# Block 1 of x normalised as columns, and a first row tile that is turned twice

## The chip, the cores and the metric

The kernel runs on one core of one Trainium2 chip. The metric is the device time of one execution in microseconds (us); lower is better. TensorE (PE) multiplies, VectorE (DVE) and ScalarE (ACT) work elementwise, GpSimd (POOL) does a few elementwise passes, and SyncE (SP) issues most of the DMA transfers; ScalarE and GpSimd issue some as well.

## The reference

An attention branch and a gated feed-forward branch run over the same normalised input, and their product is added to the input. `x` has 2048 rows of 512 numbers in f32; there are 32 heads of 16; the feed-forward width is 1792.

```python
xn = _layernorm(x, axis=-1)                       # mean and variance over the 512 columns, eps 1e-5
s  = _A_ref(xn, wqkv, wo)                         # softmax attention over all 2048 rows, then @ wo
g  = _silu(_B_ref(xn, w_gate, w_up, w_down))      # (silu(xn @ w_gate) * (xn @ w_up)) @ w_down
return x + s * g
```

## The kernel before

The kernel has an opening of some 150 us, in which `xn` and the queries, keys and values are made, and a long main part, in which attention and the feed-forward products are interleaved on TensorE by a plan written out ahead. The order on every engine is the order in which the program issues (a manual schedule); each engine's queue and each DMA queue is served in that order, and tiles carry the waits.

**Precision.** Products that need nearly full f32 use two parts: `hi`, a value rounded to fp32r, and `lo`, the rest. A product is then three products: hi by hi, lo by hi, hi by lo. So each operand of the opening is copied into a `hi` part by ScalarE and subtracted into a `lo` part by VectorE (x) or GpSimd (weights; `high_w` at L574, `low_w` at L578).

**Blocks and slots.** `x` is worked through in four blocks of 512 rows, block `b` from 0 to 3, each of four row tiles of 128 rows (`NT = 4`). A block takes twelve slots: eight feature tiles (`feature_tile`: queries and keys, 128 features by 512 rows each) and four value tiles (`value_tile`: 128 rows by 512 features). Each slot is twelve products of 128x512 on TensorE (`project`, L718 and L720) into one of four PSUM buffers `ps`, which ScalarE and VectorE empty: a feature tile as squares (`top` or `sq`, L770), `hi` (L771) and `lo` (L772), which SP's queue stores (`q_d`, `k_d`, L774) from a `parts` tile of four buffers; a value tile by a copy into `vt` (L797). In block 0 the value tiles come first (slots 0 to 3, features in slots 4 to 11); in the later blocks the feature tiles do. Slots are counted through: slot 12 is the first of block 1. The weights of a slot are loaded five slots ahead and split two slots ahead.

**Two ways to the transposed x.** The products need `xn` with its 512 columns on the partitions, in `xt[b % 2]`, as `hi` and `lo`.

- *By turning* (blocks 0 and 1 before the change): rows are loaded into `xin` (the tile `facc`), VectorE takes mean and variance (`stats`, L615 to L620), `rates` makes the reciprocal deviation `rs` (a root on ScalarE, L624, and a few tiny VectorE operations, L627 to L633), `norm` (L638) subtracts the mean and multiplies by the rate into `xn[t]`, TensorE turns it in four transposes (`turn`, L643) into a bank, `acc` or `extra`, and `split_x` takes `hi` (ScalarE, L652) and `lo` (VectorE, L655) from there. `turn_x` does turn and split.
- *By columns* (blocks 2 and 3): a second copy of `x`, already transposed, is an input (`xcols`). `columns_of` loads the block's rows for the statistics alone, and the columns themselves; `rates_x` makes means and rates; `spread_mr` turns these 8 rows with one transpose (L680), copies them (ScalarE, L681) and writes them to DRAM (`mr_d`, ScalarE's queue, L682); `load_mr` (L685) reads them back broadcast to all partitions into `wide_mr` (0.5 MB); then for each quarter of the columns VectorE subtracts and multiplies (L673), ScalarE makes `hi` and VectorE `lo` (L673 too: those are steps that the same line issues). `store_x` keeps the result in DRAM for the feed-forward part (`xt_d`, GpSimd's queue, L664).

`step(at, late, ...)` books such a piece for slot `at`, ahead of the slot's products (`late` 0) or behind them (1). The tuple given to `columns_of` holds the slots: load of rows, load of columns, statistics, rates, spread, first normalised quarter, and the delays of the `lo` parts and of the store.

**The first row tile.** To let TensorE start early, value tile 0 is not made from `hi` and `lo`, but in one pass of plain f32: row tile 0 is normalised in two halves, turned into four banks, copied to `xf` (L741) and multiplied by the raw weights (`first_tile`, L755; in the middle of it, row tile 1 is turned). `xf` is split into `xt` later, in slot 2. Ahead of it TensorE is kept busy by products of a tile of zeros (`busy`, L583). The chain of the first tile is: load, statistics, rate, normalisation, turn, copy, products.

**Copies for the feed-forward part.** `copy_fx` (L811, ScalarE) copies block 0's `xt` into `fx` in 16 pieces, one a slot.

Of the kernel before, what the change touches and what calls it, by code (L numbers as in the profile page):

```python
# [19 lines left out]
P = 128  # L20
# [99 lines left out]
def tile_block(ctx: ExitStack, tc: tile.TileContext, x, xcols, wqkv, wo, w_gate, w_up, w_down, out):  # L120
# [401 lines left out]
    with ExitStack() as pro:  # L522
# [13 lines left out]
        def load_tile(t):  # L536
            if t:
                sp.dma_start(xin[:, t % NT], x[t * P:(t + 1) * P])
            else:
                for engine, w in zip((nc.scalar, sp), wide):  # L540
                    engine.dma_start(xin[:, t, w], x[t * P:(t + 1) * P, w])

        def load_x(b):
            for t in range(NT):
                load_tile(b * NT + t)

        load_tile(0)
        busy = pc.tile([P, P], F32, name="busy")
        dve.memset(busy, 0.0)
# [29 lines left out]

        worder = [8, 9, 10, 11, 0, 1, 2, 3, 4, 5, 6, 7]  # L580

        for _ in range(11):
            mm(extra[:, :P], busy, busy, start=True, stop=True)  # L583
        for kind, i in ((load_w, 8), (load_tile, 1), (load_w, 9), (load_w, 10), (load_tile, 2), (load_w, 11),
                        (load_tile, 3), (load_w, 0)):
# [70 lines left out]

        def turn_x(b, t, between=None):
            split_x(b, t, turn(t), between)
            if t == NT - 1 and b:
                store_x(b)  # L660

        def store_x(b):
            for j in range(2):
                pool.dma_start(xt_d[b, j], xt[b % 2][j].bitcast(F32))  # L664
# [3 lines left out]
        def step(at, late, make, *what):  # L668
            steps.setdefault((at, late), []).append(partial(make, *what))
# [12 lines left out]
            nc.scalar.dma_start(mr_d[b].rearrange("s t p -> (s t) p"), rows_mr)  # L682

        def load_mr(b):
            sp.dma_start(wide_mr, mr_d[b].rearrange("s t p -> s (t p)")[None].to_broadcast([P, 2, TB]))  # L685

        def columns_of(b, rows, cols, ats):
            load, turned, counted, rated, spread, normed, lows = ats
            block = slice(b * TB, (b + 1) * TB)
            step(load, 0, sp.dma_start, rows, x[block].rearrange("(t p) d -> p t d", p=P))  # L690
            step(turned, 0, sp.dma_start, cols, xcols[:, block].rearrange("(c p) t -> p c t", p=P))
            for t in range(NT):
                step(counted + t // 2, 0, stats, t, rows)
            step(rated, 0, rates_x)
            step(spread, 0, spread_mr, b)
            step(spread + 1, 0, load_mr, b)
            hi, lo = xt[b % 2]
            for c in range(DT):
                raw = cols[:, c]
                step(normed + c, 0, dve.tensor_sub, raw, raw, wide_mr[:, 0])  # L700
                step(normed + c, 0, dve.tensor_mul, raw, raw, wide_mr[:, 1])
                step(normed + c, 1, nc.scalar.copy, hi[:, c], raw)
                step(normed + lows[c], 1, dve.tensor_sub, lo[:, c], raw, hi[:, c].bitcast(F32))
            step(normed + lows[-1], 1, store_x, b)
# [22 lines left out]


        stats(0)
        rates(0, 1)  # L730
        made = norm(0, wide)
        high_w(8)
        tc.add_manual_dep(low_w(8).ins, made.ins.name, settled, reason="GpSimd would hold VectorE up")
        xf = one.tile([P, DT, P], F32, tag="th", name="xf")
# [2 lines left out]
        for c, to in enumerate((acc, bankx, extra, banky)):  # L737
# [2 lines left out]
                rates(1, 2)  # L740
            nc.scalar.copy(xf[:, c], to[:, c * P:(c + 1) * P])  # L741
        made = norm(1)
        for c in range(1, DT):
            high_w(8 + c)
            part = low_w(8 + c)
            if c == 1:
                tc.add_manual_dep(part.ins, made.ins.name, settled, reason="GpSimd would hold VectorE up")
# [34 lines left out]
        def value_tile(b, t):  # L782
            xh, xl = xt[b % 2]
            order = None
            if b == 0:
                parts = [slice(i, i + 1) for i in range(3)] if t == 1 else [slice(0, 3, 2), slice(1, 2)]
                order = [(i, part) for part in parts for i in range(DT)]
                if t == 1:
                    order.insert(11, (partial(turn_x, 0, 2), None))
            if b == t == 0:  # L790
                ps = first_tile()
            else:
                ps = project([(vh[:, c], vl[:, c], c) for c in range(DT)], xh, xl, slice(t * P, (t + 1) * P), order,
                             extra if b == t == NB - 1 else None)
            if b == 0 and t == 1:
                turn_x(0, 3)
            nc.scalar.copy(vt5[:, :, t, :, :DH], ps.rearrange("p (g h d) -> p g h d", g=NG, h=4))  # L797
            if b < NB - 1 and t == NT - 1:
                store_v(pool, b, 0, NT)
            elif b == NB - 1 and t == 1:  # L800
                store_v(sp, b, 0, 2)
            elif b == NB - 1 and t == NT - 1:
                return partial(store_v, sp, b, 2, NT)
# [6 lines left out]
            dst = fx[halves[h], j].rearrange("p (c u) t -> u p c t", u=2)[u]  # L810
            nc.scalar.copy(dst[:, 2 * w:2 * w + 2], xt[0][j][halves[u], 2 * w:2 * w + 2])  # L811

        columns_of(2, raw_x, raw_x, (7, 12, 10, 12, 14, 19, (1, 2, 3, 3)))
        columns_of(3, xin, raw_x, (11, 24, 15, 24, 26, 31, (1, 2, 3, 3)))

        for b in range(NB):
            more = b + 1 < NB
            slots = [(feature_tile, m) for m in range(8)]
            slots = [(value_tile, t) for t in range(NT)] + slots if b == 0 else slots + [(value_tile, t) for t in range(NT)]
            for n, (make, i) in enumerate(slots):  # L820
                if b == 0:
                    if n + 5 < 12:
                        load_w(worder[n + 5])
                    if n >= 2 and n + 2 < 12:
                        high_w(worder[n + 2])
                        low_w(worder[n + 2])
                if not b and n == 2:
                    load_x(1)
                run_steps(12 * b + n, 0)
                if b == 2 and n in (6, 7):  # L830
                    load_gu(n - 6)
                if b == 2 and n == 8:
                    load_wd(0)
                if not more and n == 2:
                    split_gu(0)
                    dve.memset(acc, 0.0)
                if not more and n in (1, 3):
                    load_k(0, n // 2)
                if not more and n == 5:
                    load_q(0)  # L840
                if not more and n == 6:
                    for c in range(2):
                        load_v(0, c)
                if b == 0 and n == 1:
                    norm(2)
                    norm(3)
                if not b and 6 <= n < 10:
                    norm(n - 6)
                made = make(b, i)
                if not more and n == 8:  # L850

                    for m in range(8):
                        squares(m, top[m])
                    for j in range(2):
                        dve.reduce_max(peak[:, j:j + 1], banks[j], axis=AX.X)
                    dve.tensor_add(sm, peak[:, 0:1], peak[:, 1:2])
                if b == 0 and n == 2:
                    split_x(0, 0, xf)
                if b < 2 and 0 <= 12 * b + n - 3 < 16:
                    copy_fx(12 * b + n - 3)  # L860
                if b == 0 and n == 11:
                    ring(0, 2, one)
                    queries(0, one)
                    for h in range(2):
                        pool.memset(qst[0][h * HALF:h * HALF + 2].bitcast(F32), 0.0)
                run_steps(12 * b + n, 1)
                if not b:
                    for t in range(NT):
                        if n == 2 + t // 2:
                            stats(t)  # L870
                    if n == 4:
                        rates(0, NT)
                    if 7 <= n < 11:
                        turn_x(1, n - 7)
                if not more and n == 9:
                    tops = pps.tile([P, 512], F32, tag="ps", name="tops")
                    nc.tensor.transpose(tops[0:1, :P], sm, ident)
                    dve.reduce_max(s4, tops[0:1, :P], axis=AX.X)
                    dve.tensor_scalar(s4, s4, 0.51, None, op0=ALU.mult)
                    dve.tensor_scalar(flag, s4, LIMIT, None, op0=ALU.is_le)  # L880
                    dve.tensor_scalar(shift, row, s4, -1.0, op0=ALU.add, op1=ALU.mult)
                    sp.dma_start(s_d, shift.bitcast(F32))
                    for h in range(2):
                        sp.dma_start(qst[0][h * HALF:h * HALF + 1].bitcast(F32), shift.bitcast(F32)[:, None].to_broadcast([1, 2, 512]))
                    pool.dma_start(sh_d[:NG * NB].rearrange("u (j t) -> (u j) t", t=TB), s_d.to_broadcast([NG * NB * 4, TB]))
                    fill(3 * DC)
                    fast = nc.values_load(flag, min_val=0, max_val=1)
# [212 lines left out]
```

## Time and profile before

| | us |
|---|---|
| median of 3 runs (lowest to highest) | 1385.10 (1385.07 to 1385.13) |
| the profiled execution, its own time | 1385.12 |
| its span in the profile | 1383.3 |
| TensorE busy | 1377.5 |
| ScalarE busy | 1158.2 |
| VectorE busy | 775.9 |
| GpSimd busy | 103.5 |

The span goes from the first to the last instruction of the core; the execution's own time has 1.8 us more around it. Times inside the profile are counted from the span's start. A row of the timeline has the start, the duration, the engine, the line, the operation, output and inputs with their shapes, a count, and in brackets the idle time ahead of it and what ended that. A row of the stretches has, behind the stretch, the busy time of TensorE, its weight loads, VectorE, ScalarE and GpSimd with their counts, the granted TensorE clock, the busy share of the DMA engines, and GB/s. `ACTq` and `SPq` are the issuing of transfers from those queues. A plain f32 product shows as two instructions, a product of fp32r operands as one.

### The profile page before, as it was taken

Reading aid. Unit: us, or ns where it says so; the run is one execution under the profiler, and the core shown is the slowest. Engines: PE = TensorE matmul, PEld = TensorE weight load, DVE = VectorE, ACT = ScalarE, POOL = GpSimd, SP = SyncE. Lnnn points to the kernel's source line nnn. Section 1 sums busy time; section 2 is a strip of 40 time slices with the busy share of each in tenths; the row PEclk is TensorE's granted clock in tenths of the full one; section 3 lists DMA queues with packets and bytes.
Section 4 is the critical chain, followed back from the end, with each engine's and each line's share of the span. In section 5 each row is a group of like instructions: output and inputs, shape, how many; then the busy total and the mean of one; then the engine's idle time right before and its main releaser. Section 6 shows DMA issues by size and latency. Waiting matters only on the chain.

```text
span 1383.3 us, 27675 instructions
## 1 busy us (share of the span) xinstructions
PE 1377.5 (100%) x11167; PEld 868.4 (63%) x11167; DVE 775.9 (56%) x1250; ACT 1158.2 (84%) x1943; POOL 103.5 (7%) x145
## 2 busy tenths in 40 slices
PE   9999999999999999999999999999999999999998
PEld 7787666656655665565566555566566556655665
DVE  6655466365545663565465643655466545655656
ACT  6644589888888898899998988888888888899875
POOL 4200100000010000000110000000100000000142
PEclk9999999999999999999999999999999999999999
DMA  7989541134553511233724402356333312234752
GB/s 238 307 283 297 147 106 44 36 77 106 111 128 82 135 44 36 51 90 86 173 56 115 110 13 51 74 127 145 83 78 83 101 25 59 59 86 133 226 188 84
DMA packets 132260, 154.71 MB, mean 112 GB/s; under 512 B 13489, under 2 KB 83137, under 8 KB 131358
## 3 DMA queue, kind: packets, MB, share of 16 engines
q1 hardware_dynamic: 124782, 128.03, 36.1%
q0 software_dynamic: 6880, 24.32, 5.2%
q8 instruction: 89, 1.46, 0.5%
q10 hardware_dynamic: 464, 0.53, 0.1%
q14 instruction: 45, 0.37, 0.1%
HBM read 110.61 MB, written 40.12 MB: 109 GB/s over the span
## 4 chain that ended last, share of the span: by engine, by line
PE 89%; DVE 0%; DVEq 0%; issue 0%
PE acc L450 33%; PE bankx L244 29%; PE score L981 10%; PE single L981 8%; PE banky L244 7%; PE spare L981 1%; PE spare L1036 0%; PE banky L1036 0%; DVE y L1043 0%; PE score L1036 0%; PE single L1036 0%; DVE y L1049 0%; DVEq L1096 0%
## 5 line engine op out<-in xcount | busy, mean ns | idle before, releaser
L450 PE MATMUL acc<-pr,vst 128*17 128x512 f32 x4096 | 459.3, 593 | 0.0
L991 ACT ACTIVATE pr<-single 128x512 f32<-128x512 f32 x762 | 429.3, 604 | 17.2 <-PE single L981 0.5
L984 ACT ACTIVATE pr<-score 128x1024 f32<-128x1024 f32 x318 | 327.9, 1031 | 87.1 <-PE score L981 84.3
L450 PEld LDWEIGHTS acc<-pr,vst 128*17 128x17 f32 x4096 | 115.6, 97 | 279.5 <-issue 275.3
L244 PE MATMUL banky<-fx,guh 64*128 64x512 f32 x896 | 290.8, 392 | 0.0
L244 PE MATMUL bankx<-fx,guh 64*128 64x512 f32 x896 | 290.5, 391 | 0.1
L988 DVE COPY pr<-spare 128x512 f32<-128x512 f32 x194 | 134.1, 691 | 182.5 <-PE spare L981 169.6
L981 PE MATMUL score<-qst,kst 50*128 50x512 f32 x830 | 218.8, 418 | 0.0
L981 PE MATMUL single<-qst,kst 50*128 50x512 f32 x922 | 212.6, 398 | 0.0
L244 PE MATMUL banky<-wd,hh 64*128 64x512 f32 x672 | 196.0, 391 | 0.0
L244 PE MATMUL bankx<-wd,hh 64*128 64x512 f32 x672 | 195.9, 391 | 0.0
L1001 ACT ACTIVATE pr<-pr 128x512 f32<-128x512 f32 x354 | 193.3, 641 | 0.0
L244 PEld LDWEIGHTS bankx<-fx,guh 64*128 64x128 f32 x896 | 166.8, 186 | 21.4 <-DVE guh L205 0.6
L244 PE MATMUL bankx<-fx,gul 64*128 64x512 f32 x448 | 175.6, 392 | 0.0
L244 PE MATMUL banky<-fx,gul 64*128 64x512 f32 x448 | 175.5, 392 | 0.0
L981 PEld LDWEIGHTS score<-qst,kst 50*128 50x128 f32 x830 | 98.9, 184 | 112.9 <-ACT pr L991 69.2
L244 PEld LDWEIGHTS banky<-fx,guh 64*128 64x128 f32 x896 | 166.9, 186 | 1.1
L991 ACT ACTIVATE pr<-score 128x512 f32<-128x512 f32 x194 | 116.9, 603 | 35.5 <-PE spare L981 27.7
L988 DVE COPY pr<-single 128x512 f32<-128x512 f32 x160 | 110.5, 691 | 59.1 <-PE single L981 49.3
L244 PEld LDWEIGHTS bankx<-wd,hh 64*128 64x128 f32 x672 | 125.1, 186 | 17.8
L981 PEld LDWEIGHTS single<-qst,kst 50*128 50x128 f32 x922 | 114.8, 184 | 23.0 <-ACT pr L991 7.6
L244 PEld LDWEIGHTS banky<-wd,hh 64*128 64x128 f32 x672 | 125.1, 186 | 5.9
(191 smaller groups left out, 1689.9 us busy)
## 6 DMA issues: line engine op xcount, KB each, us to landing
gur<-in_B_w_gate_dram SPq DMA_DIRECT2D x56, 256.0 KB
gur<-in_B_w_up_dram SPq DMA_DIRECT2D x56, 256.0 KB
wdr<-in_B_w_down_dram SPq DMA_DIRECT2D x56, 256.0 KB
kst<-k_d SPq DMA_DIRECT2D x192, 64.0 KB
qst<-q_d SPq DMA_DIRECT2D x192, 64.0 KB
fx<-xt_d SPq DMA_DIRECT2D x24, 512.0 KB
q_d<-parts SPq DMA_DIRECT2D x16, 512.0 KB
k_d<-parts SPq DMA_DIRECT2D x16, 512.0 KB
```

The source lines that it names most:

```text
L244: mm(bank, lhs[h], rhs[h], start=start, stop=stop)
L450: mm(acc[h * 32:h * 32 + DH + 1], v[:, kt % CT, h * (DH + 1):(h + 1) * (DH + 1)], probs[2 * i + h // 2][:, h % 2], start=kt == 0, stop=kt ...
L981: mm(banked[h], k[r, j, kc * P:(kc + 1) * P], q[r, j], start=True, stop=True)
L984: exps.append(act(pr, both_banks, AF.Exp, scale=0.25))
L988: dve.tensor_copy(pr[:, h], banked[h])
L991: exps.append(act(pr[:, h], banked[h], AF.Exp, scale=0.25))
L1001: exps.append(act(part, part, AF.Exp, scale=0.25))
```

## The change

1. **First row tile.** Ahead of the first turn only its mean is subtracted. Its rate is made later (`rates(0, 1)` behind the normalisation of row tile 1) and multiplied in when value tile 0 is copied out of PSUM. For the `hi` and `lo` parts the tile is normalised again in slot 1, and turned a second time behind slot 2. The products of zeros ahead of it go from 11 calls to 9.
2. **Block 1** goes the way of the columns: rows into `raw_x` (slot 1), columns into `xin` (slot 2), statistics in slots 2 and 3, rates behind slot 3, spread ahead of slot 5, normalised from slot 7 on. Its turns, normalisations and loads of row tiles go. Its broadcast is issued on GpSimd's queue, behind slot 5's products.
3. **Blocks 2 and 3**: the loads, and block 2's statistics, rates and spread, come two slots later; the normalisation of block 2 stays at slot 19. `copy_fx` starts one slot later.

```diff
-        def load_x(b):
-            for t in range(NT):
-                load_tile(b * NT + t)
...
-        for _ in range(11):
+        for _ in range(9):
             mm(extra[:, :P], busy, busy, start=True, stop=True)
...
         def turn_x(b, t, between=None):
             split_x(b, t, turn(t), between)
-            if t == NT - 1 and b:
-                store_x(b)
...
         def load_mr(b):
-            sp.dma_start(wide_mr, mr_d[b].rearrange("s t p -> s (t p)")[None].to_broadcast([P, 2, TB]))
+            (pool if b == 1 else sp).dma_start(wide_mr, mr_d[b].rearrange("s t p -> s (t p)")[None].to_broadcast([P, 2, TB]))
...
-            step(rated, 0, rates_x)
+            step(rated, b == 1, rates_x)
             step(spread, 0, spread_mr, b)
-            step(spread + 1, 0, load_mr, b)
+            step(*((spread, 1) if b == 1 else (spread + 1, 0)), load_mr, b)
...
         stats(0)
-        rates(0, 1)
-        made = norm(0, wide)
+        xn[0] = two.tile([P, D], F32, tag="ga", name="xn")
+        for w in wide:
+            made = dve.tensor_scalar(xn[0][:, w], xin[:, 0, w], mv[:, 0, 0:1], None, op0=ALU.subtract)
...
         made = norm(1)
+        rates(0, 1)
...
             if b == 0 and t == 1:
                 turn_x(0, 3)
-            nc.scalar.copy(vt5[:, :, t, :, :DH], ps.rearrange("p (g h d) -> p g h d", g=NG, h=4))
+                norm(0)
+            dst, src = vt5[:, :, t, :, :DH], ps.rearrange("p (g h d) -> p g h d", g=NG, h=4)
+            if b == t == 0:
+                act(dst, src, AF.Copy, scale=rs[:, 0:1])
+            else:
+                nc.scalar.copy(dst, src)
...
-        columns_of(2, raw_x, raw_x, (7, 12, 10, 12, 14, 19, (1, 2, 3, 3)))
-        columns_of(3, xin, raw_x, (11, 24, 15, 24, 26, 31, (1, 2, 3, 3)))
+        columns_of(1, raw_x, xin, (1, 2, 2, 3, 5, 7, (1, 1, 2, 3)))
+        columns_of(2, raw_x, raw_x, (9, 14, 12, 14, 16, 19, (1, 2, 3, 3)))
+        columns_of(3, xin, raw_x, (13, 24, 17, 24, 26, 31, (1, 2, 3, 3)))
...
-                if not b and n == 2:
-                    load_x(1)
...
-                if not b and 6 <= n < 10:
-                    norm(n - 6)
...
                 if b == 0 and n == 2:
-                    split_x(0, 0, xf)
-                if b < 2 and 0 <= 12 * b + n - 3 < 16:
-                    copy_fx(12 * b + n - 3)
+                    turn_x(0, 0)
+                if b < 2 and 0 <= 12 * b + n - 4 < 16:
+                    copy_fx(12 * b + n - 4)
...
-                if not b:
-                    for t in range(NT):
-                        if n == 2 + t // 2:
-                            stats(t)
-                    if n == 4:
-                        rates(0, NT)
-                    if 7 <= n < 11:
-                        turn_x(1, n - 7)
```

## The prediction

> **What bounds the kernel now.** I read the page first (engine shares, the chain of waits), then the timeline of TensorE through the opening 150 us, then those of the other engines, the stretches of 10 us, and the waits of the DMA queues.
>
> ```profile
> span 1383.3 us, 27675 instructions
> ...
> PE 1377.5 (100%) x11167; PEld 868.4 (63%) x11167; DVE 775.9 (56%) x1250; ACT 1158.2 (84%) x1943; POOL 103.5 (7%) x145
> ...
> PE 89%; DVE 0%; DVEq 0%; issue 0%
> ```
>
> The chain that ended last lies on TensorE, which is idle for 5.8 us of the 1383.3. So a microsecond that TensorE starts earlier, or that is struck off its queue, shortens the run by as much, and one that it waits lengthens it, unless a later wait absorbs it. Busy ends are modelled, so I take the starts of the products instead:
>
> ```profile
> 20.61 0.63 PE L718 MATMUL ps<-xt,wh 128*128 128x512 f32 x2
> ...
> 44.71 1.00 PE L718 MATMUL ps<-xt,wh 128*128 128x512 f32 x2
> 45.55 0.39 PE L718 MATMUL ps<-xt,wl 128*128 128x512 f32 x1
> ...
> 67.58 0.63 PE L720 MATMUL ps<-vh,xt 128*128 128x512 f32 x2
> ...
> 78.78 0.63 PE L718 MATMUL ps<-xt,wh 128*128 128x512 f32 x2
> ```
>
> These are the first products of slots 4, 12, 20 and 24 (twelve slots to a block of 512 rows, twelve products to a slot). Slots 20 to 23 last 11.20 us, 2.80 a slot, 0.233 a product, with no gap. Everything else between two such rows is an extra, and the extras are what the change touches.
>
> **The change part by part.**
>
> *The turns of block 1 go.* From 20.61 to 44.71 is 24.10 us; eight slots are 22.40. The rest, 1.70, is four turns (four transposes each) at 0.425. They leave the queue: -1.70.
>
> *Tile 0 is turned a second time*, after slot 2: one more turn, +0.43. It has until slot 4: the copy on ScalarE and the subtraction on VectorE that follow it fit into slot 3 (2.80).
>
> *One transpose of the means and rates for block 1* comes before slot 5. Block 2 shows its price:
>
> ```profile
> 50.45 0.40 PE L718 MATMUL ps<-xt,wl 128*128 128x512 f32 x1
> 50.68 0.27 PE L680 MATMUL extra<-ident,mr 128*8 128x128 f32 x1
> 50.71 0.71 PE L718 MATMUL ps<-xt,wh 128*128 128x512 f32 x2
> 51.25 0.40 PE L718 MATMUL ps<-xt,wl 128*128 128x512 f32 x1
> ...
> 26.40 1.30 POOL L578 TENSOR_TENSOR wl<-wraw,wh 128x512 fp32r<-128x512 f32 x1 [2.17 <-ACT wh L574]
> 26.92 0.80 DVE L633 SCALAR_TENSOR_TENSOR mr<-nw,mr 128x4 f32<-128x4 f32 x1
> ...
> 48.88 0.16 DVE L633 SCALAR_TENSOR_TENSOR mr<-nw,mr 128x4 f32<-128x4 f32 x1
> ```
>
> From 50.45 to 51.25 stand three products (0.70) and the transpose: +0.10. But TensorE stands behind it in order, and it needs the rates. Their last step takes 0.16 alone and 0.80 at 26.92, where it ended at 27.72, just after GpSimd's subtraction at 27.70. By my order of VectorE (statistics of the rows, the second half of tile 0, then rates once slot 3's copy is out) that step comes at about 22.7, while GpSimd subtracts from 22.3 to 23.6; TensorE wants the result at 23.4. Bounds: 0 (not held) to +0.8 (held, and the statistics a little late); I take +0.35.
>
> [...]
>
> *The wait at slot 12.* From 44.71 to 67.58 is 22.87, eight slots and 0.47 more. 0.10 is the transpose; 0.37 is the pause between 44.71 and 45.55, where the third product stands behind
>
> ```profile
> 44.47 0.69 DVE L655 TENSOR_TENSOR xt<-extra,xt 128x512 fp32r<-128x512 f32 x1 [0.33 <-ACT xt L652]
> ```
>
> which ends at 45.16 and is the low half of block 1's last row tile. With columns, slot 12 needs the last quarter only at its tenth product, so this wait goes: -0.37, at worst 0.
>
> *The head.* The first turn no longer waits for the rate.
>
> ```profile
> 1.07 5.07 PE L583 MATMUL extra<-busy 128*128 128x128 f32 x22 [1.07 <-DVE ind L590]
> 4.19 0.21 DVE L620 BATCH_NORM_AGGREGATE mv<-st 128x2 f32<-128x12 f32 x1
> 5.47 0.73 DVE L638 TENSOR_SCALAR xn<-facc,mv,mr 128x256 f32<-128x256 f32 x2
> 6.03 0.45 PE L643 MATMUL acc<-ident,xn 128*128 128x128 f32 x1
> 6.91 0.81 PE L755 MATMUL ps<-wraw,xf 128*128 128x512 f32 x1
> 7.56 1.02 PE L755 MATMUL ps<-wraw,xf 128*128 128x512 f32 x2
> 7.99 1.02 PE L755 MATMUL ps<-wraw,xf 128*128 128x512 f32 x2
> ```
>
> VectorE ends the statistics at 4.40 and starts on the tile at 5.47; without the rate it can start at about 4.45, 1.0 earlier. The eleven warm-up calls are 22 instructions from 1.07 to 6.03, 0.225 each; two calls fewer take 0.90 from them. So the first transpose can start at 5.13 in place of 6.03, and the first product at 6.01. Not all of this is kept. The first plain f32 product takes 0.65 (6.91 to 7.56), the second, of the same shape, 0.43 (7.56 to 7.99), though neither is shown to wait. I read that as TensorE running at half rate until about 7.36: 0.45 at half rate and 0.20 at full rate make one product of 0.43. (The page's row of the granted clock shows full speed all along.) If that moment stays, the products spend 1.35 us at half rate in place of 0.45 and lose 0.45 more: -0.90 + 0.45 = -0.45. The rate of tile 0, now behind tile 1's normalisation, takes VectorE the 1.0 that it took before, so tiles 2 and 3 come about as they did. Bounds: -0.90 (half rate ends earlier by as much) and -0.2 (a weight or a tile is late).
>
> [...]
>
> *Block 1 as columns.* Removed: four loads of row tiles, four normalisations, four copies and subtractions from PSUM. Added: one load of 1 MB of rows early, 1 MB of columns behind slot 1's second normalisation of tile 0 on SP's queue (only two weights, needed three slots later, stand behind it), the 4 KB write of means and rates on ScalarE's queue, the 0.5 MB broadcast on GpSimd's, and on VectorE two passes per quarter in place of one. The question is when the broadcast lands.
>
> ```profile
> 25.71 0.61 ACT L574 CAST wh<-wraw 128x512 fp32r<-128x512 f32 x1
> 53.21 0.52 ACTq L682 DMA_DIRECT2D mr_d<-busy  x1
> 59.11 0.33 SPq L685 DMA_DIRECT2D wide_mr<-mr_d  x1
> 142.45 0.35 SPq L882 DMA_DIRECT2D s_d<-shift  x1
> 145.83 0.56 POOL L885 DMA_DIRECT2D sh_d<-s_d  x1 [31.31 <-DMA s_d<-shift]
> sh_d<-busy POOLq DMA_DIRECT2D x1, 256.0 KB, 4.3
> v_d<-vt POOLq DMA_DIRECT2D x1, 1088.0 KB, 5.3
> 71.88 1.41 DVE L673 TENSOR_TENSOR raw_x<-raw_x,wide_mr 128x512 f32<-128x512 f32 x2
> 79.34 1.46 DVE L673 TENSOR_TENSOR xt<-raw_x,xt 128x512 fp32r<-128x512 f32 x2
> 20.00:30.00 10.00, 10.00 (x45) 8.05 (x44) 6.53 (x18) 8.31 (x14) 5.24 (x5) 1.00 0.68 218
> 50.00:60.00 10.00, 10.00 (x45) 7.98 (x44) 3.80 (x9) 4.97 (x9) 1.84 (x2) 1.00 1.05 370
> 140.00:150.00 10.00, 10.00 (x68) 7.56 (x67) 4.16 (x8) 2.48 (x3) 0.56 (x1) 1.00 0.70 193
> ```
>
> ScalarE reaches the small copy behind slot 5's weight (25.71 + 0.61) and issues the write at about 26.6. A small write has been seen to free its reader after 3.4 us (142.45 to 145.83) and after 5.9 (53.21 to 59.11). GpSimd then issues, and its transfers land after 4.3 (0.25 MB) to 5.3 (1 MB). So the broadcast is there between 26.6 + 3.4 + 4.3 = 34.3 and 26.6 + 5.9 + 5.3 = 37.8. Block 2's columns take VectorE from 71.88 to 80.80, 8.9 us, with one feature subtraction of 0.69 among them; here four stand among them, so 11.0: ready between 45.3 and 48.8. TensorE's slot 12 begins at 44.71 - 0.45 + 0.43 + 0.45 - 1.70 = 43.4 and wants the last low quarter at its eleventh product, 45.7. So the wait is 0 to 3.1, and 1.3 more if one GpSimd subtraction holds VectorE: bounds 0 to +4.4. I take the faster write, because the DMA engines' share at 20 to 30 us, 0.68, is nearer to the 0.70 of the stretch of the 3.4 than to the 1.05 of that of the 5.9 (the last column but one), and, for the chance of a hold (45.3 + 1.3 is 0.9 past 45.7), about half of that: +0.5.
>
> What waits behind that wait: on GpSimd, the low half of slot 8's weights. At the early end GpSimd is free at 30.0, issues by 30.6 and ends the subtraction at 31.9, before slot 8's third product at 32.7; at the late end 34.7, a wait of 2.0 which overlaps the one above. On ScalarE and VectorE, the feature tiles' copies; four PSUM buffers leave them three slots.
>
> *The DMA engines, and blocks 2 and 3 two slots later.* 1.5 MB more are moved.
>
> ```profile
> 60.88 0.59 ACT L771 CAST parts<-ps 128x512 fp32r<-128x512 f32 x1 [3.70 <-DMA k_d<-parts]
> 66.59 0.69 DVE L772 TENSOR_TENSOR parts<-ps,parts 128x512 fp32r<-128x512 f32 x1 [2.45 <-ACT parts L771]
> ```
>
> The extra columns fall where the share is 0.68. At 50 to 70 the engines are full: ScalarE waits 3.7 us for a store, and the PSUM buffer freed at 67.28 is used at 67.58, a margin of 0.3. But the two loads of 1 MB that stood ahead of those stores are issued two slots later, behind two more stores. I take 0; bounds 0 to +3.8 (1.5 MB at the 370 GB/s of 50 to 60 us is 4.1 us, less the margin).
>
> *The rest* (ScalarE's scaled copy in place of a plain one, copies to fx one slot later, statistics moved) replaces like by like off TensorE: 0, covered by TensorE's unbroken slots.
>
> **Sum:** -1.70 + 0.43 + 0.10 + 0.35 - 0.37 - 0.45 + 0.5 = -1.14 us. The profiled execution took 1385.12 with a span of 1383.3; 1385.12 - 1.14 = 1384.0, and from the median, 1385.10, it is the same. The best ends, without the DMA term, give -0.90 + 0.43 - 1.70 + 0.10 - 0.37 = -2.4 (1382.7); the worst -0.2 + 0.43 - 1.70 + 0.10 + 0.8 + 4.4 = +3.8 (1388.9).
>
> **The rivals.**
>
> *The columns come late; the gain is given back.* The broadcast lands at 36 to 37.8, and slot 12 waits 1.5 to 4.4 us instead of 0.37. For it: the 5.9 us write, and two transfers one after the other across queues. Against: the share of 0.68. Without the columns' wait the sum is -1.64, so the middle of this case is 1385.1 - 1.6 + 3 = 1386.5. From a wait of 1.6 on, a broadcast at 36.3 without a hold or 35.0 with one, it is slower than before; over 0.2% slower (2.8 us) needs a wait of 4.4, a broadcast at 37.8 with one hold or 39.1 without.
>
> *The stores are pushed back.* The extra 1.5 MB reaches the full stretch after 50 us and TensorE waits for PSUM: up to 1385.1 - 1.1 + 3.8 = 1387.8; from 1.1 on it is slower than before. For it: the margin of 0.3. Against: the loads moved behind the stores.
>
> *The earlier start is wholly kept and nothing waits:* 1382.7. Against: the 0.65 us product.
>
> *The head brings nothing*, since the earlier work only runs at half rate or waits for its weights: 1384.0 + 0.45 = 1384.4.
>
> **How the numbers follow.** Forecast, with the head bringing nothing in it (1382.9 to 1384.8): 0.60. Columns late, up to 0.2% slower: 0.20. Columns later still: 0.06. Stores pushed back: 0.08, half of it over 0.2%. All kept: 0.06, half of it over 0.2% faster with some wait gone that I haven't seen. 0.2% is 2.8 us, about what a measurement of this kernel can tell from no change. Faster 0.03; slower 0.06 + 0.04 = 0.10; same 0.87. The range 1382.8 to 1386.4 takes in the forecast and most of the late columns.
>
> **What would show each step.** The first transpose near 5.1 and the first two products about 0.86 apart (head); slot 4 near 20.6; no transposes of row tiles after slot 2; the transpose before slot 5 at about 23.7, after a held step on VectorE; the broadcast's first reader on VectorE near 34.3; slot 12 at 43.4 and its eleventh product's wait under 1 us; slot 20 about 1.2 us ahead of 67.58, with ScalarE's waits for stores no longer than before. Wrong it would be if TensorE pauses in slots 8 to 12 or 16 to 24 by more than 1 us, or if the shift at slot 24 isn't carried to the end.

## The result, and the profile after

The changed kernel is slower: 1393.02 us (1392.70 to 1393.59) against 1385.11 (1384.84 to 1385.18), a ratio of 1.0058 [1.0048, 1.0069]. That is outside the predicted range of 1382.8 to 1386.4. The execution profiled took 1393.59, with a span 8.5 us longer than that of before. Line numbers of the changed kernel lie 4 to 10 below those of the kernel before (L712 is the former L718, L667 the former L673).

From the page of the changed kernel:

```profile
span 1391.8 us, 27654 instructions
...
PE 1378.7 (99%) x11152; PEld 867.4 (62%) x11152; DVE 779.2 (56%) x1256; ACT 1157.4 (83%) x1944; POOL 104.1 (7%) x146
...
PE 88%; issue 0%; DVE 0%; DVEq 0%
```

TensorE has 15 instructions fewer (11167 before), which is what the change promised, and is idle for 13.1 us instead of 5.8. Its timeline shows where. Each row ends with the idle time before it and who ended it:

```profile
9.82 1.20 PE L714 MATMUL ps<-vh,xt 128*128 128x512 f32 x4
12.10 1.19 PE L714 MATMUL ps<-vh,xt 128*128 128x512 f32 x4 [1.08 <-DVE ve L623]
21.22 0.63 PE L712 MATMUL ps<-xt,wh 128*128 128x512 f32 x2
24.63 0.27 PE L674 MATMUL extra<-ident,mr 128*8 128x128 f32 x1 [0.45 <-DVE mr L629]
39.44 0.73 PE L712 MATMUL ps<-xt,wh 128*128 128x512 f32 x2 [0.52 <-ACT wh L570]
41.32 0.50 PE L712 MATMUL ps<-xt,wl 128*128 128x512 f32 x1 [1.15 <-POOL wl L574]
49.38 0.50 PE L712 MATMUL ps<-xt,wh 128*128 128x512 f32 x1 [0.22 <-DVE xt L667]
78.63 0.73 PE L714 MATMUL ps<-vh,xt 128*128 128x512 f32 x2 [0.45 <-DVE parts L768]
82.83 0.50 PE L712 MATMUL ps<-xt,wh 128*128 128x512 f32 x1 [0.20 <-DVE xt L667]
84.76 0.50 PE L712 MATMUL ps<-xt,wh 128*128 128x512 f32 x1 [0.97 <-DVE xt L667]
158.30 0.47 PE L971 MATMUL score<-qst,kst 50*128 50x512 f32 x1
160.93 0.47 PE L971 MATMUL score<-qst,kst 50*128 50x512 f32 x1 [2.15 <-issue]
163.03 1.00 PE L971 MATMUL score<-qst,kst 50*128 50x512 f32 x2
165.59 0.61 PE L971 MATMUL score<-qst,kst 50*128 50x512 f32 x2
```

The last four rows lie behind the branch that leads from the projections to the main part. The same pairs of score products before, without a stop:

```profile
153.68 0.70 PE L981 MATMUL score<-qst,kst 50*128 50x512 f32 x2
155.64 0.60 PE L981 MATMUL score<-qst,kst 50*128 50x512 f32 x2
157.43 0.51 PE L981 MATMUL score<-qst,kst 50*128 50x512 f32 x2
```

The first pair starts at 153.68 before, 158.30 after (+4.62). After, its second product comes only at 160.93. The second pair is 7.39 late (155.64, 163.03), the third 8.16 (157.43, 165.59). Two stretches of 2 us show the rest; the third number from the end is the granted clock:

```profile
162.00:164.00 2.00, 2.00 (x14) 1.79 (x12) 0.00 (x0) 1.49 (x3) 0.84 (x1) 0.55 1.15 239
164.00:166.00 2.00, 2.00 (x14) 1.80 (x12) 0.00 (x0) 1.93 (x3) 1.89 (x3) 0.59 0.32 67
```

Stops are counted from start to start, less 0.233 a product, with the slower product just behind each (0.1). The prediction's terms against what the trace has, in us:

| term | predicted | trace |
|---|---|---|
| head and second turn of tile 0 (start of slot 4: 20.61 to 21.22) | -0.45 + 0.43 | +0.61 |
| four turns of block 1 gone | -1.70 | -1.70 |
| transpose of the rates, before slot 5 | +0.10 + 0.35 | +0.78 |
| old wait at slot 12 gone | -0.37 | -0.37 |
| block 1's columns late | +0.5 | +2.81 (slot 10: 2.21; slot 12: 0.60) |
| blocks 2 and 3 booked later | 0 | +2.43 (slot 23: 0.71; slot 24: 1.72) |
| sum at the first score product | -1.14 | +4.56 (the starts: +4.62) |
| stop behind the branch, half rate after it | none | +2.40, +1.1 |

With 0.4 over the long rest, that makes the 8.5. The rows of the other engines that stand behind the waits:

```profile
5.91 0.69 DVE L611 BATCH_NORM_STATS2 st<-facc 128x6 f32<-128x512 f32 x1 [0.90 <-DMA facc<-in_A_x_dram]
8.57 3.74 POOL L574 TENSOR_TENSOR vl<-wraw,vh 128x512 fp32r<-128x512 f32 x3 [2.15 <-DVE mr L624]
8.91 0.95 DVE L629 SCALAR_TENSOR_TENSOR mr<-nw,mr 128x1 f32<-128x1 f32 x1
23.25 1.29 POOL L574 TENSOR_TENSOR wl<-wraw,wh 128x512 fp32r<-128x512 f32 x1
23.30 1.28 DVE L629 SCALAR_TENSOR_TENSOR mr<-nw,mr 128x4 f32<-128x4 f32 x1
26.92 0.52 ACTq L676 DMA_DIRECT2D mr_d<-busy  x1
30.72 0.57 POOL L679 DMA_DIRECT2D wide_mr<-mr_d  x1 [2.60 <-DMA mr_d<-busy]
36.80 1.42 DVE L667 TENSOR_TENSOR facc<-facc,wide_mr 128x512 f32<-128x512 f32 x2 [4.41 <-DMA wide_mr<-mr_d]
38.25 0.62 ACT L667 CAST xt<-facc 128x512 fp32r<-128x512 f32 x1 [2.73 <-DVE facc L667]
38.77 0.61 ACT L570 CAST wh<-wraw 128x512 fp32r<-128x512 f32 x1
39.47 1.80 POOL L574 TENSOR_TENSOR wl<-wraw,wh 128x512 fp32r<-128x512 f32 x1 [4.72 <-ACT wh L570]
63.72 0.27 ACTq L676 DMA_DIRECT2D mr_d<-busy  x1
68.64 0.33 SPq L679 DMA_DIRECT2D wide_mr<-mr_d  x1
76.56 1.42 DVE L667 TENSOR_TENSOR raw_x<-raw_x,wide_mr 128x512 f32<-128x512 f32 x2 [3.56 <-DMA wide_mr<-mr_d]
```

Read the chain of slot 10 from 26.92 on. ScalarE issues the small write, 3.8 us later GpSimd can issue the broadcast, and 6.1 us after that VectorE's first pass begins. Meanwhile ScalarE is stuck: the cast of block 1's first quarter (38.25) stands in its queue ahead of the cast of slot 10's weight (38.77), so TensorE waits at 39.44 for the one half of that weight and at 41.32 for GpSimd's other half. The wait that I had looked for at slot 12 came two slots sooner, through a weight that has nothing to do with the columns but queues behind them.

### The profile page after: what moved, and what is told of

Its sections match the earlier page's. It is cut to its first block, busy times and chain, and to the rows that moved or that the text cites. A ratio compares the mean times of both kernels' runs of the same rounds, so it can differ in the third digit from the quotient of the medians.

```text
span 1391.8 us, 27654 instructions
## 1 busy us (share of the span) xinstructions
PE 1378.7 (99%) x11152; PEld 867.4 (62%) x11152; DVE 779.2 (56%) x1256; ACT 1157.4 (83%) x1944; POOL 104.1 (7%) x146
## 3 DMA queue, kind: packets, MB, share of 16 engines
q8 instruction: 90, 1.47, 0.5%
## 4 chain that ended last, share of the span: by engine, by line
PE 88%; issue 0%; DVE 0%; DVEq 0%
PE acc L450 32%; PE bankx L244 30%; PE score L971 10%; PE single L971 8%; PE banky L244 6%; PE spare L971 1%; PE spare L1026 0%; PE banky L1026 0%; DVE y L1033 0%; PE score L1026 0%; PE single L1026 0%; DVE y L1039 0%; DVEq L1086 0%
```

## The experiments

Times are medians; where the kernel before ran beside them it stood at 1384.9 to 1385.1. Rows are from one execution each, the profiled one, and executions of one kernel differ here by up to 3.6 us. The theory after the first reading: four separate causes (head, columns of block 1, block 2's later bookings, the stop behind the branch), each of which can be taken away alone. The general rival: one cause, such as the fuller DMA engines, behind them all.

**The stop: 15 instructions put back.**

```diff
+                if b == 2 and n == 6:
+                    for _ in range(15):
+                        mm(extra[:32, :4], ind, ind[:, :4], start=True, stop=True)
```

> The changed kernel with 15 tiny extra products (32x4) on TensorE in slot 30, so that as many TensorE instructions stand ahead of the branch to the main part as before the change. Theory (the 2.6 us pause just after the branch and the half rate behind it come from where the branch's target lies in TensorE's instruction stream, so that an instruction fetch is waited for): the pause goes, 1393.0 - 2.4 - 1.6 + about 0.5 for the products = 1389.5. Rival (the pause comes from the store of values or the weights' loads that are issued at that moment): the pause stays, 1393 to 1394.

Measured: 1390.74, ratio 1.0041 [1.0027, 1.0056]. The stop and the half rate behind it are gone, the pairs are 1.97 apart as before (1.96):

```profile
160.52 0.69 PE L974 MATMUL score<-qst,kst 50*128 50x512 f32 x2
162.49 0.60 PE L974 MATMUL score<-qst,kst 50*128 50x512 f32 x2
```

Products that compute nothing made the kernel 2.3 us faster, though they take 0.56 us themselves (a figure of the run with all causes taken away, below). The waits of slots 10 and 24 ahead of the branch stayed. In the profiled execution, at 1392.17 the slowest of the five, half rate came behind the wait of slot 10 instead:

```profile
44.00:46.00 2.00, 2.00 (x6) 1.58 (x5) 2.00 (x2) 1.98 (x4) 1.29 (x1) 0.50 0.67 241
```

There each of seven products took 0.19 us more than 0.233. So half rate is not tied to the branch.

**The head alone, in the kernel before; and the change without its head.** The first keeps block 1 as row tiles and all bookings of before. The second keeps the columns and takes the first tile's turn back:

```diff
-        xn[0] = two.tile([P, D], F32, tag="ga", name="xn")
-        for w in wide:
-            made = dve.tensor_scalar(xn[0][:, w], xin[:, 0, w], mv[:, 0, 0:1], None, op0=ALU.subtract)
+        rates(0, 1)
+        made = norm(0, wide)
...
-                    turn_x(0, 0)
+                    split_x(0, 0, xf)
```

> The kernel before with the first-row-tile part of the change alone (mean only ahead of the first turn, 9 warm-up calls, rate behind tile 1, second turn in slot 2); block 1 still turned. Theory (the 1.1 us won at the first products is lost again where TensorE waits for tile 1's low half, because VectorE now makes the rate in between and is held by GpSimd): +0.2 and the second turn +0.43, so 1385.7; as many TensorE instructions as before, so no pause after the branch. Rival (the head's gain of 0.45 is kept and the loss lies elsewhere): 1385.1 or below.

> The changed kernel with the first row tile as before the change (rate ahead of the turn, 11 warm-up calls, split from xf): the columns of block 1 and the moved bookings alone. Theory (most of the loss is here): waits in slots 10 and 12 of about 2.7 us in sum, in slots 23 and 24 about 2.4, the pause after the branch about 4 (15 TensorE instructions fewer, as in the change), against 1.7 + 0.37 saved and 0.6 for the spread: 1392.4 to 1392.8. Rival (the head's shift is what makes the columns late): under 1390.

Measured: the head alone 1386.09, ratio 1.0006 [0.9997, 1.0016]: no gain, a loss of 1.0 that hardly stands out. The change without its head 1391.91 (1391.16 to 1393.21), 1.0053 [1.0036, 1.0070], 1.1 below the change, though the runs of the two overlap. From the head alone:

```profile
6.61 0.69 DVE L615 BATCH_NORM_STATS2 st<-facc 128x6 f32<-128x512 f32 x1 [1.53 <-DMA facc<-in_A_x_dram]
12.81 1.19 PE L720 MATMUL ps<-vh,xt 128*128 128x512 f32 x4 [1.08 <-DVE ve L627]
```

and from the change without its head, where slot 4 starts a little earlier than before, but the stop is there all the same:

```profile
20.36 0.62 PE L712 MATMUL ps<-xt,wh 128*128 128x512 f32 x2
...
159.78 0.46 PE L964 MATMUL score<-qst,kst 50*128 50x512 f32 x1 [1.73 <-issue]
```

In all eleven kernels with the new head and its order of rates (the changed one, the head alone and nine others of this section), slot 4 starts 15.31 to 15.33 us behind the start of tile 1's statistics, whether that lies at 5.30 or at 6.95. So with the new head it is tile 1 that sets the time, and the earlier products only wait sooner (row 12.10). Where tile 1 had landed in time, slot 4 starts where it did before (20.61); this is the changed kernel with 30 tiny products in slot 30:

```profile
5.30 0.70 DVE L611 BATCH_NORM_STATS2 st<-facc 128x6 f32<-128x512 f32 x1
20.62 0.63 PE L712 MATMUL ps<-xt,wh 128*128 128x512 f32 x2
```

**The held rate moved.** The rate of tile 0 goes behind the rates of tiles 2 and 3, out of the way of tile 1's low half.

> The changed kernel with the first row tile's rate made behind row tile 1's split, together with the rates of tiles 2 and 3. Theory (in the head, VectorE's five small steps for that rate, one of them held by GpSimd, 1.4 us in all, delay tile 1's low half and TensorE waits 1.1 for it): the wait at the fifth product of slot 1 goes, -1.1: 1391.9. Rival (row tile 1's load sets the end whatever the order): unchanged, 1393.

Measured: 1393.67, 1.0061 [1.0045, 1.0078]; the rival was right. The wait passes to the next thing that VectorE makes, and slot 4 still starts 15.13 us behind tile 1's statistics, 0.18 sooner than with the rate where the change has it:

```profile
14.13 0.66 PE L639 MATMUL acc<-ident,xn 128*128 128x128 f32 x4 [0.76 <-DVE xn L634]
```

**Blocks 2 and 3: bookings of before, and one slot in between.** The first puts (7, 12, 10, 12, 14, 19) and (11, 24, 15, 24, 26, 31) back, the second has 8, 13, 11, 13, 15 and 12, 24, 16.

> The changed kernel with blocks 2 and 3 booked as before the change (loads, statistics, rates and spread two slots earlier). Theory (the waits of slots 23 and 24 come from block 2's broadcast being issued two slots later): these waits of 2.4 us go, the others stay, 1390.6. Rival (block 2's statistics and loads now collide with block 1's late columns on VectorE and the DMA engines): the wait at slot 12 grows by 1 to 3 us and the time stays at 1392 or above.

> The changed kernel with the steps of blocks 2 and 3 booked one slot earlier than it has them (one slot later than the kernel before). Theory: the waits in slots 23 and 24 (0.61, 0.37 and 1.14 us in the changed kernel) come from the columns of block 2 standing late on VectorE; they shrink from 2.1 to 1 us or less, slot 12 stays at about 0.6, as block 2's statistics still stand behind block 1's last low quarter: 1391.5 (1390.8 to 1392.2). Rival, as when the bookings of before were put back: what slots 23 and 24 give, slot 12 takes, and the time stays at 1392.5 to 1394.

Measured: 1393.97, 1.0065 [1.0048, 1.0081] with the old bookings; 1390.66, 1.0041 [1.0027, 1.0054] with those in between. Both take the waits of slots 23 and 24 away (0.3 and nothing left). So those came from the bookings. With the old ones slot 12 pays 1.91 instead, and the trace names it: two tiles of block 2's statistics stand on VectorE ahead of the last low quarter of block 1.

```profile
49.20 0.69 DVE L611 BATCH_NORM_STATS2 st<-raw_x 128x6 f32<-128x512 f32 x1
...
51.40 0.68 DVE L667 TENSOR_TENSOR xt<-facc,xt 128x512 fp32r<-128x512 f32 x1
...
52.13 0.50 PE L712 MATMUL ps<-xt,wh 128*128 128x512 f32 x1 [1.66 <-DVE xt L667]
```

With the bookings in between the last low quarter comes first and slot 12 stays at 0.50; 0.67 is lost anew at the transpose of block 2's rates. 1393.02 to 1390.66 is 2.4, more than I had expected, but the five runs spread from 1389.53 to 1393.12, so the size is uncertain; that the two waits go is read from the trace.

**The broadcast.** On SP's queue instead of GpSimd's; then read from two rows of x, so that it doesn't wait for the write (its values are then not the means and rates); then the weights split three slots ahead instead of two.

```diff
-            (pool if b == 1 else sp).dma_start(wide_mr, mr_d[b].rearrange("s t p -> s (t p)")[None].to_broadcast([P, 2, TB]))
+            src = x[:2] if b == 1 else mr_d[b].rearrange("s t p -> s (t p)")
+            (pool if b == 1 else sp).dma_start(wide_mr, src[None].to_broadcast([P, 2, TB]))
...
-                    if n >= 2 and n + 2 < 12:
-                        high_w(worder[n + 2])
-                        low_w(worder[n + 2])
+                    for m in (4, 5) if n == 2 else (n + 3,) if 2 < n < 9 else ():
+                        high_w(worder[m])
+                        low_w(worder[m])
```

> The changed kernel with block 1's broadcast issued on SP's queue instead of GpSimd's. Theory (the lateness comes from the write that must land first and from full DMA engines, not from the queue): the first reader on VectorE starts within 1.5 us of 36.8, time within 1 us of 1393. Rival A (GpSimd's queue is what makes it slow, 6.1 us to land): reader near 35, 1391. Rival B (SP's queue is worse, behind a store): reader near 39, 1395.

> The changed kernel with block 1's broadcast read from two rows of x instead of the means and rates (so that block 1 is normalised with wrong numbers): nothing waits for the write any more; the small copies and the write are still made. Theory (the lateness of the broadcast is the whole of the waits of slots 10 and 12): the first reader starts when the program comes to it, near 32, and 2.7 us go: 1390.3. Rival (VectorE's and ScalarE's added passes are too many for slots 7 to 11 anyway, held by GpSimd's weight subtractions): slot 12 still waits 1 us or more, 1391.5 or above.

> The changed kernel with the weights of slots 5 to 11 split three slots ahead instead of two. Theory (slot 10 waits because ScalarE stands at block 1's first high quarter, which waits for the late broadcast, and the high half of slot 10's weights stands behind it): the waits of slot 10 (0.69 + 1.41 us) go, but the broadcast is as late, so part of them comes back at slot 12: 1391.5 to 1393. Rival (slot 10's wait is all that the columns cost): 1390.9.

Measured: on SP 1392.56, 1.0057 [1.0040, 1.0074]: issue 30.56, first reader 36.71, 6.15 us against 6.1, so the queue doesn't matter here. Without the wait for the write 1390.26, 1.0041 [1.0026, 1.0055]: issued 3.2 us earlier, read 3.1 earlier (0.5 of each comes from the head of that execution, whose slot 4 starts at 20.72), and the waits of slot 10 are gone:

```profile
27.55 0.57 POOL L680 DMA_DIRECT2D wide_mr<-in_A_x_dram  x1
33.67 1.85 DVE L667 TENSOR_TENSOR facc<-facc,wide_mr 128x512 f32<-128x512 f32 x2 [1.78 <-DMA wide_mr<-in_A_x_dram]
```

Weights further ahead 1391.41, 1.0047 [1.0030, 1.0064]: the waits of slot 10 are gone here too, with the broadcast as late as ever, and slot 12 pays 1.15 and 0.49. So slot 10 waited for its weight, and the weight for the columns: either end of that chain, taken away, frees the slot.

**What the stop hangs on.** Three, nine and thirty tiny products instead of 15; the kernel before with 4 warm-up products instead of 11 (14 TensorE instructions fewer, nothing else changed); and the kernel before with three tiny products more.

> The changed kernel plus three tiny TensorE products (32x4 by 32x32) in slot 30, well ahead of the branch; they compute nothing that is used. The changed kernel has 15 TensorE instructions fewer ahead of the branch than the kernel before, and stops for 2.15 us after five products behind the branch; with 15 tiny products added the stop was gone. Theory that the stop is tied to the instruction's place in TensorE's program: the stop stays and comes after two products instead of five, at about the same length (1.7 to 2.4 us), time 1392.5 to 1393.5. Rival, that the stop is tied to the work (the fifth product behind the branch waits for something): it comes after five products again. Second rival, that any shift of the program removes it: no stop, and about 1391.

> The changed kernel plus 9 tiny products in slot 30. With none added the stop came after five products behind the branch, with 3 after four, with 15 there was none. Theory that the stop stands at a fixed distance in TensorE's program: after two products, 1.7 to 2.4 us, time 1391.5 to 1393.5. Rival, that it depends on the work: four or five products again, or none.

> The changed kernel plus 30 tiny products in slot 30. Theory: the place at which TensorE would stop has moved ahead of the branch, as with 15, and there is no stop behind it, time 1390.5 to 1392 (0.5 more for the products than with 15). Rival, that the places come at short equal distances: a stop again, some products behind the branch.

> The kernel before with 4 warm-up products at the head instead of 11: 14 TensorE instructions fewer ahead of the branch, 15 in the changed kernel; nothing else is changed. Theory: it gets the changed kernel's stop, of 1.7 to 2.4 us about five products behind the branch, with or without 1.6 us of half rate behind it; with a head that is up to 1 us slower for its shorter warm-up, 1387 to 1389.5. Rival, that the stop comes from the changed kernel's order and waits: no stop, 1385 to 1386.

> The kernel before plus 3 tiny products in slot 30. Theory: the place of the stop lies ahead of the branch in the kernel before, and 3 more products move it further ahead: no stop, 1385.2 (0.1 us for the products). Rival, that the kernel before stands just at a place where any shift brings a stop: 1387 to 1389.

Measured: with 3, 1393.13, the stop is there, one product sooner (not three, as expected). With 9 (1390.47) and 30 (1389.80) there is none; for 9 that was a miss. These two and the next two are single runs. The kernel before with fewer warm-up products gets the stop at the same product as the changed kernel, and takes 1390.35; with three more products it doesn't (1385.51). From the kernel before with 4 warm-up products:

```profile
155.64 0.46 PE L981 MATMUL score<-qst,kst 50*128 50x512 f32 x1
157.70 0.62 PE L981 MATMUL score<-qst,kst 50*128 50x512 f32 x1 [1.59 <-issue]
```

Its first score product is 1.96 late, all of it a slower head; its span is 5.3 longer, so 3.3 come from the stop and the half rate after it (granted clock 0.50 from 159 to 161 us). So it is the number of TensorE instructions ahead of the branch that decides, not the columns or their waits. Nor is it a late branch: with the head alone the first score product is 1.33 late, with 15 tiny products 6.84, and neither stops.

The queues of instruction transfers may bear on how. The page after has

```profile
q8 instruction: 90, 1.47, 0.5%
```

That is 90 transfers of 16.3 KB. I take the queue as TensorE's: it moves 1.47 of the 1.84 MB of both instruction queues, and TensorE has 22304 of the 27654 instructions, products and weight loads. In all ten kernels that stop the page counts 90 of them, in all eight that don't, 89. Found in half-microsecond windows, as distances from the first product behind the branch:

| kernel | stop | transfers on this queue, us |
|---|---|---|
| before | no | -18.5, -3.5, -0.5, +12.0 |
| changed | yes | -12.5, -3.5, 0, +5.5 |
| changed + 3 | yes | -13.0, -3.5, -0.5, +5.5 |
| changed + 9 | no | -13.0, -3.5, 0, +13.5 |
| changed + 15 | no | -18.5, -3.0, 0, +11.5 |
| before, 4 warm-ups | yes | -12.5, -3.5, -0.5, +5.5 |

Two transfers stand around the branch in every kernel, at -3.5 to -3.0 and at -0.5 to 0. Where TensorE stops, the next comes at +5.5 already; where it doesn't, at +11.5 or later. So the transfers go with the stop; that TensorE waits for one of them is my guess and is shown by no run, and the shift by one product for three added is not explained.

**All causes taken away.** Old head; block 1 as columns with its spread and broadcast half a slot earlier; weights three slots ahead; the bookings in between for blocks 2 and 3; fx copies one more slot later; 15 tiny products in slot 30. Then the same with the tiny products in the head.

```diff
-            step(spread, 0, spread_mr, b)
-            step(*((spread, 1) if b == 1 else (spread + 1, 0)), load_mr, b)
+            step(*((spread - 1, 1) if b == 1 else (spread, 0)), spread_mr, b)
+            step(*((spread, 0) if b == 1 else (spread + 1, 0)), load_mr, b)
```

> The changed kernel with all the named causes taken away at once: the first row tile turned once, as in the kernel before, with its head; block 1 of x still from the column copy, but its spread and the load of its broadcast each half a slot earlier; the weights split three slots ahead instead of two; blocks 2 and 3 booked one slot earlier; the copies of x's halves one slot later; 15 tiny products in slot 30. Theory (the four turns of block 1 were worth 1.7 us and all the rest were waits that order can remove): no stop behind the branch, no wait at slot 10, at most 1 us in slots 12 and 24 together: 1385.3 (1384.3 to 1386.5), so level with the kernel before, or a little faster. Rival, the broadcast is bound by its 6.1 us of landing and the waits only move to slots 9 to 12: 1387 to 1389.

> The kernel with all the named causes taken away, with its 15 tiny products moved from slot 30, where they take 0.56 us of TensorE's path (94.32 to 94.78 and a seam of 0.10), to the head, between the warm-up products (ended at 5.42 us) and the first transpose (6.04 us, waiting for VectorE), where TensorE is idle for 0.62 us. Theory: the stop behind the branch depends on how many TensorE instructions stand ahead of it and not on where they stand, so it stays away, and the 0.56 us are saved: 1384.0 (1383.6 to 1384.4). Rival: the products in the head push the first transposes back by some tenths, and the time stays at 1384.5. Second rival: the place of the 15 matters, the stop comes back, and the time is 1386 to 1388.

Measured: 1384.52 (1384.20 to 1384.80), 0.9996 [0.9987, 1.0005]; then 1383.98 (1383.67 to 1384.25), 0.9992 [0.9983, 1.0001]. From 20 us to the branch TensorE waits once, at the transpose of the rates (0.46). In the first of the two the broadcast is issued 3.3 us earlier than in the changed kernel:

```profile
27.38 0.57 POOL L679 DMA_DIRECT2D wide_mr<-mr_d  x1
33.22 1.85 DVE L667 TENSOR_TENSOR facc<-facc,wide_mr 128x512 f32<-128x512 f32 x2 [1.52 <-DMA wide_mr<-mr_d]
```

The last kernel's runs lie below all runs of the kernel before (1384.91 to 1385.44), by 1.1 us in the median, though the interval still touches 1. The tiny products in its head did push the first transposes to 6.55, as the rival had it, but only 0.23 of that was left at slot 4, and its stop stayed away. So the columns bring a gain, once the order around them is right. Its size is near the forecast's 1.14 in part by luck: what is left is -1.70 - 0.37 for the turns and the old wait, +0.7 for the transpose and +0.2 for the head, about -1.2, while the forecast had 0.45 for the transpose and 0.5 for late columns. The general rival is out: the padding, the bookings and the weights or the broadcast each took away their own wait and left most of the others, and the last two kernels move the columns' bytes without the waits.

## Why the prediction was wrong

**The turns, right.** -1.70 and the old wait's -0.37 came as worked out, and the last two kernels show them kept.

**The transpose of the rates, right in kind.** The last step on VectorE was held to 1.28 (0.16 alone) beside GpSimd's 1.29 (rows 23.25 and 23.30), as the upper bound had it; 0.78 in place of 0.45.

**The head, wrong in sign.** The failed step is that tile 1 was as good as taken to be there once VectorE was early: the bound for a late tile was -0.2, and the head without the second turn cost +0.18 (0.61 - 0.43). VectorE found tile 1 missing by 0.90 (row 5.91), and all that follows starts from there. Where tile 1 was there at 5.30, slot 4 starts at 20.62, beside the forecast's 20.6; the changed kernel has both 0.6 later. "Takes VectorE the 1.0 that it took before" was wrong too: the rate took 1.4, with the last step held to 0.95, and tile 1's low half, which TensorE wants next, stood behind it. But moving it on won only the 0.18, so it is not what sets the time. Being early at the first product moved the wait to the fifth product of slot 1. The sum's -0.45 took it that half rate ends at 7.36 in the changed kernel too; no run shows that, nor the term. The first four transposes there start 0.18, 0.11 and 0.10 us apart from 5.07 on, against 0.24, 0.21 and 0.22 before (and 0.22, 0.21 and 0.21 in the run with three tiny products, whose head is the same); the page's granted clock is 1.00 from 5 to 9 us in both kernels. What the runs showed in its place is the +0.18. So the -0.45 had the wrong reason, and that 20.6 comes out with tile 1 in time is luck.

**The columns, mis-sized and misplaced.** +0.5 was 2.81. The broadcast's first reader came at 36.80, inside my 34.3 to 37.8. But I took the early end, by the DMA engines' share: the write took 3.8, the landing 6.1, more than both rows that I had (4.3 and 5.3). And I looked at slot 12 alone. I did name GpSimd's subtraction behind the broadcast, but not that ScalarE's cast of a quarter, which waits for VectorE, stands ahead of the cast of slot 10's weight. The rival "columns late" is what happened in this part.

**Blocks 2 and 3 later, taken as 0, was 2.43.** I argued from the bytes on the DMA engines. The failed step is that I never asked for the reader of the broadcast: load, statistics and spread move by two slots, the first pass over the columns stays booked at slot 19. Before, VectorE's first pass at 71.88 showed no wait; now it waits 3.56 us for a broadcast issued 9.5 later, and slots 23 and 24 with it. The rival of pushed stores had the right stretch, after 50 us, and the wrong cause.

**The stop behind the branch was in none of the forecast's cases.** With the half rate after it, it cost 3.5 of the 8.5. The failed step is the first one, that a microsecond struck off TensorE's queue "shortens the run by as much": instructions struck off that queue brought a stop of 2.40 and 1.1 of half rate. The count of TensorE instructions, which the prediction used only as a saving, also decides here whether TensorE stops behind the branch (14 fewer brought the stop, 9 more took it away). How it does so stays open.

## What to carry to other kernels

When a step is moved, follow it to its first reader and then to everything that queues behind that reader on each engine: here the wait for the columns showed up at slot 10's weight, which was next in ScalarE's queue (0.52 idle at 39.44, 1.15 at 41.32). Before an edit is judged, look for a stop that the profile puts down to "issue" just behind a branch; if there is one, shift the program by some ten instructions (here three were too few, nine were enough) and measure again, or the edit is charged with time that isn't its own, here 3.3 to 3.5 us. An earlier start was worth nothing here (first product at 5.76 in place of 6.91, slot 4 at 21.22 in place of 20.61), since the next load didn't land earlier too.

## What the runs showed of the hardware

- A stop of 1.59 to 2.15 us behind the branch came with 14 or 15 TensorE instructions fewer ahead of it, stayed with three tiny products added, and went with 9, 15 and 30.
- After that stop the granted clock fell to about one half for some 3 us in some kernels (0.60, 0.50, 0.50 and 0.69 in the four microseconds from 162 to 166 of the changed one; 0.50 from 159 to 161 with 4 warm-up products), and not in others, though the stops were much the same (1.59 with 4 warm-up products; 1.73 in the change without its head, at a clock of 1.00 from 157 to 167). With 15 tiny products it fell to 0.50 behind the waits of slot 10 (44 to 46). What sets it is not shown.
- A broadcast of 0.5 MB took 6.1 us to its reader from GpSimd's queue, 6.15 from SP's, and 6.1 when it read two rows of x instead. It took 5.8 in the kernel with the causes taken away, and block 2's, on SP's queue, 7.9 in the changed kernel (rows 68.64 and 76.56).
- A step on VectorE that takes 0.16 us alone (7.69 in the changed kernel, 48.88 in the one before) took 0.95 and 1.28 beside a GpSimd subtraction of 1.25 and 1.29 (rows 8.91 and 23.30).
